# Splitting the first weight load of a decode-attention kernel into one third and the rest

## The chip, the cores and the metric

The kernel runs on one core of a Trainium2 chip. The metric is the device time of one execution in microseconds. A profiled execution also has a span (243.8 us for the kernel before), from its first to its last instruction; it is some 1.5 us shorter than the time. The profile's names: PE is the matmul engine and PEld its weight load, DVE, ACT and POOL are the other compute engines, SP issues the large loads. A load *lands* when its last byte is there. A ratio is the mean time of one kernel's fast runs over that of the other's in the same rounds on the same chip, so it is not quite the ratio of the medians that are quoted.

## The reference, cut to what matters

Two independent attention layers, A and B, decode one token each. A attends to the last 2048 positions of its cache, B to all 8192.

```python
Hq, Hkv, Sk, Dh = 32, 16, 8192, 128          # x has 576 elements
q = (x @ wq)                                  # wq: 576 x 4096
k, v = caches, each of 16 heads repeated for 2 query heads   # A: last 2048 rows only
p = softmax(q @ k.T * Dh ** -0.5)
out = (p @ v) @ wo                            # wo: 4096 x 576
# result: concatenate([A, B])
```

There is one query row per head, so there is little to compute for each byte: the inputs that must be read are 102.8 MB.

## The kernel before

All large inputs are loaded by one queue (SP), in a fixed order: wq of A, wq of B, keys and values of A, then keys and values of B in four groups, then wo of A and of B. The buffers are reused, so later loads wait until PE has read what stood there. wq of A is one load: 128 partitions, and in each one run of 18,432 elements (36,864 bytes).

```python
    def load(dst, src, writes, dma):
        add("sp", lambda sp: sp.dma_start(dst, src()), writes=writes, dma=dma)
    ...
    def q_part(P, off, res):                  # the projection x @ wq: 36 matmuls
        def mm(pe):
            for u in range(9):
                for j in range(4):
                    o = off + u * 2048 + j * 512
                    ins = pe.matmul(...rhs=slots[:, o:o + 512], start=(u == 0), stop=(u == 8))
            return ins
        add("pe", mm, reads=[("xpad", P)] + res, ...)     # waits for all of res first
    ...
    for P in range(2):                        # 0 is A, 1 is B
        off, res = WQ[P]
        x_columns(P)
        load(slots[:, off:off + WQ_W], lambda P=P: wqs[P]..., res, "wq%d" % P)
        q_part(P, off, res)
        q_finish(P)
```

The very first load of the program is moved ahead of the barrier with which the engines start together; all other loads are issued behind it:

```python
        first = per["sp"].pop(0)
        ...
        lead.insert(at, ins)                  # before the barrier
```

Of the kernel before, what the change touches and what calls it, by code (L numbers as in the profile page):

```python
# [20 lines left out]
WQ_W = 18432  # L21
# [15 lines left out]
class Program:  # L37
# [15 lines left out]
    def add(self, eng, fn, reads=(), writes=(), dma=None, after=(), tag=None, inc=1, loop=None):  # L53
        op = Op(eng, fn, tuple(reads), tuple(writes), dma, tag, inc if dma is None or inc > 1 else 16, loop)
        deps = []
        for r in op.reads:
            w = self.writer.get(r)
            if w is not None:
                deps.append((w, True))
            if r[0] == "bank":  # L60
                deps += [(o, False) for o in self.readers.get(r, ())]
        for r in after:
            deps += [(o, False) for o in self.readers.get(r, ())]
        for r in op.writes:
            w = self.writer.get(r)
            if w is not None:
                deps.append((w, False))
            deps += [(o, False) for o in self.readers.get(r, ())]
        for r in op.reads:
            self.readers.setdefault(r, []).append(op)  # L70
        for r in op.writes:
            self.writer[r] = op
            self.readers[r] = []
        for o, raw in deps:
            if o is op:
                continue
            if o.dma is None and o.eng == eng and (not raw or eng in ("pe", "sp")):
                continue
            op.deps.append(o)
            o.needed = True  # L80
        op.order = len(self.ops)
        self.ops.append(op)
        return op
# [192 lines left out]
def bass_concat_heads__sliding_block_cached__gqa_block_cached__decode_kernel(  # L276
# [16 lines left out]
    wqs = [A_wq, B_wq]  # L293
# [16 lines left out]
    slots = nc.alloc_sbuf_tensor("slots", [128, 4 * SLOT], BF16)  # L310
# [86 lines left out]
    def load(dst, src, writes, dma):  # L397
        add("sp", lambda sp: sp.dma_start(dst, src()), writes=writes, dma=dma)  # L398
# [49 lines left out]
    def x_columns(P):  # L448
        for u, n, col, i, e in ((0, 5, 0, 0, 0), (0, 5, 1, 4, 1), (1, 4, 0, 5, 1), (1, 4, 1, 0, 0)):
            dst = bass.AP(tensor=xpad, offset=(P * 9 + u) * 32 + col, ap=[[576, 128], [64, n]])  # L450
            add("dve", lambda dve, dst=dst, o=320 + 9 * P + i, n=n, e=e: dve.tensor_scalar(
                dst, misc[:, o:o + n], par2[:, e:e + 1], None, ALU.mult),
                reads=[B_M, "par2"], writes=[("xpad", P)])

    def q_part(P, off, res):
# [4 lines that stand above are left out]
                    ins = pe.matmul((turned if P else opsum)[32 * j:32 * j + 32, :], lhsT=xpad[:, P, u, :],  # L460
                                    rhs=slots[:, o:o + 512], start=(u == 0), stop=(u == 8))
            return ins
        add("pe", mm, reads=[("xpad", P)] + res, writes=[B_T if P else B_O])

    def q_finish(P):
        add("act", lambda act: act.activation(qrow[:, :], (turned if P else opsum)[:, :], ACT.Copy),  # L466
            reads=[B_T if P else B_O], writes=["qrow"])

        def tr(pe):
            for i in range(4):  # L470
                ins = pe.matmul(misc[:, i * 8:(i + 1) * 8], lhsT=qrow[:, i * 128:(i + 1) * 128],  # L471
                                rhs=selq[:, :, :].rearrange("p j h -> p (j h)"), start=True, stop=True)
            return ins
        add("pe", tr, reads=["qrow", "selq"], writes=[B_M])
        add("dve", lambda dve: dve.tensor_copy(qcol[:, P, :].rearrange("p (h j i) -> p i j h", h=2, j=4),  # L475
                                               misc[:, 0:32].rearrange("p (i j h) -> p i j h", i=4, j=4)),
            reads=[B_M], writes=[("qcol", P)])
# [236 lines left out]
    for P in range(2):  # L714
        off, res = WQ[P]
        x_columns(P)
        load(slots[:, off:off + WQ_W], lambda P=P: wqs[P].rearrange("(m r) n -> m (r n)", m=64)
             .rearrange("m (e y) -> (m e) y", e=2), res, "wq%d" % P)
        q_part(P, off, res)
        q_finish(P)  # L720

    sums(kindA[:, :].rearrange("p (b y) -> p b y", b=4), identf[:, :].rearrange("p (a b c y) -> p b y a c", a=2, b=4, c=2),
# [96 lines left out]
```

## Time and profile before

| what | value |
|---|---|
| time, median of 3 runs | 245.35 us (245.17 to 245.45) |
| span of the profiled run | 243.8 us |
| bytes moved | 102.88 MB, 422 GB/s over the span |
| share of the span in which the load queue's packets run | 98.3% |
| busiest compute engine | PE, 67% |

Compare the share of the load queue with that of the busiest engine: 98 against 67.

### The profile page before, as it was taken

The page shows a single profiled execution, that of the slowest core. Times are in us where ns is not written, and L with a number is a line of the kernel's source. Part 1 is how long each engine was busy: PE and PEld are TensorE (multiplying, and loading weights), DVE is VectorE, ACT ScalarE, POOL GpSimd, SP SyncE. Part 2 cuts the span into 40 slices and gives each one's busy share as a digit, 9 for nine tenths or more (in the row PEclk, how much of TensorE's full clock was granted, in tenths as well). Part 3 has the DMA queues.
Part 4 walks back from the last instruction along what each step waited for, and adds up shares of the span by engine and source line. Part 5 has one row for each costly group of instructions (what it writes and reads, how often), then busy time and mean ns, then how long its engine had stood idle before and what let it go on. Part 6 is the DMA issues. An engine that isn't in the chain of part 4 may idle for free. (4 is left out here: it accounts for less than half of the span.)

```text
span 243.8 us, 5219 instructions
## 1 busy us (share of the span) xinstructions
PE 164.0 (67%) x2328; PEld 119.3 (49%) x2328; DVE 88.2 (36%) x152; ACT 93.2 (38%) x96; POOL 6.8 (3%) x34
## 2 busy tenths in 40 slices
PE   0060739957249997393999452999457699944966
PEld 0020239744217784233887220987233688634854
DVE  0101127866205655203556312456322255534031
ACT  2000017855304776202778300678600368730000
POOL 6001000000000000000000000000000000000000
PEclk9999967999759999569899859799957589985599
DMA  9999999999999999899999999999989999989994
GB/s 351 424 442 403 430 433 422 430 425 427 449 427 433 485 398 462 371 435 430 485 409 452 419 403 435 435 489 398 473 366 430 435 489 419 462 374 423 422 406 175
DMA packets 3968, 102.88 MB, mean 422 GB/s; under 512 B 500, under 2 KB 632, under 8 KB 888
## 3 DMA queue, kind: packets, MB, share of 16 engines
q1 hardware_dynamic: 3896, 102.76, 98.3%
q8 instruction: 6, 0.10, 0.2%
q10 hardware_dynamic: 64, 0.00, 0.0%
q14 instruction: 2, 0.02, 0.0%
HBM read 102.76 MB, written 0.00 MB: 422 GB/s over the span
## 5 line engine op out<-in xcount | busy, mean ns | idle before, releaser
L510 ACT ACTIVATE kt<-ktps 128x1024 bf16<-128x1024 bf16 x80 | 79.8, 1042 | 87.5 <-PE ktps L500 87.3
L500 PE MATMUL ktps<-ident,slots 128*128 128x128 bf16 x1280 | 86.0, 231 | 19.9 <-PEq L214 17.4
L500 PEld LDWEIGHTS ktps<-ident,slots 128*128 128x128 bf16 x1280 | 79.8, 104 | 35.5 <-issue 35.4
L513 DVE COPY kt<-ktps 128x1024 bf16<-128x1024 bf16 x80 | 60.8, 774 | 54.5 <-PE ktps L500 54.5
L592 PE MATMUL opsum<-slots,ptm 128*32 128x512 bf16 x320 | 27.0, 510 | 13.4 <-PEq L214 13.4
L525 PE MATMUL sacc<-kt,qst 128*32 128x512 bf16 x320 | 25.4, 392 | 2.3 <-PEq L214 2.3
L592 PEld LDWEIGHTS opsum<-slots,ptm 128*32 128x32 bf16 x320 | 13.5, 124 | 25.5 <-issue 22.6
L563 PE MATMUL misc<-ident,psb 128*128 128x128 bf16 x40 | 4.7, 290 | 15.8 <-PEq L214 15.8
L610 DVE TENSOR_TENSOR vtmp<-opsum,maskV 128x512 f32<-128x512 f32 x4 | 2.8, 692 | 32.4 <-PE opsum L592 32.4
L551 ACT ACTIVATE psb<-sacc,stat 128x2048 bf16<-128x2048 f32 x5 | 9.8, 1967 | 9.7 <-DVE stat L540 9.7
L563 PEld LDWEIGHTS misc<-ident,psb 128*128 128x128 bf16 x40 | 3.5, 128 | 18.2 <-issue 18.2
L570 DVE TENSOR_TENSOR ptm<-misc,maskP 128x1024 bf16<-128x1024 bf16 x5 | 3.5, 691 | 16.1 <-PE misc L563 16.1
L525 PEld LDWEIGHTS sacc<-kt,qst 128*32 128x32 bf16 x320 | 5.0, 94 | 8.4 <-issue 4.7
L707 ACT ACTIVATE outsb<-ktps 64x144 bf16<-64x144 f32 x1 | 0.3, 287 | 20.2 <-PE ktps L695 20.2
L460 PE MATMUL turned<-slots,xpad 128*32 128x512 bf16 x36 | 4.0, 630 | 5.9 <-DMA slots<-in_B_wq_dram 5.9
L441 PE MATMUL misc<-xnine,twice 16*128 16x18 bf16 x4 | 0.3, 171 | 11.0 <-DMA xnine<-in_B_x_dram 11.0
L695 PE MATMUL ktps<-slots,opj 128*32 128x144 bf16 (+1 forms) x192 | 6.7, 247 | 0.8 <-issue 0.7
L475 DVE CAST qcol<-misc 128x32 bf16<-128x32 f32 x2 | 0.6, 300 | 17.2 <-PE misc L471 17.2
L695 PEld LDWEIGHTS ktps<-slots,opj 128*32 128x32 bf16 x192 | 5.4, 96 | 2.0 <-issue 0.9
L485 POOL COPY qst<-qcol 128x32 bf16<-128x32 bf16 x8 | 1.7, 211 | 152.2 <-PE sacc L525 152.2
L466 ACT ACTIVATE qrow<-opsum 128x512 bf16<-128x512 f32 x1 | 0.6, 597 | 13.8 <-PE opsum L460 13.8
L460 PE MATMUL opsum<-slots,xpad 128*32 128x512 bf16 x36 | 4.0, 630 | 2.6 <-DMA slots<-in_A_wq_dram 2.6
(77 smaller groups left out, 56.9 us busy)
## 6 DMA issues: line engine op xcount, KB each, us to landing
slots<-in_B_k_cache_dram SPq DMA_DIRECT2D x8, 4096.0 KB
slots<-in_A_k_cache_dram SPq DMA_DIRECT2D x4, 2048.0 KB
slots<-in_A_v_cache_dram SPq DMA_DIRECT2D x4, 2048.0 KB
slots<-in_A_wq_dram SPq DMA_DIRECT2D x1, 4608.0 KB, 13.9
slots<-in_B_wq_dram SPq DMA_DIRECT2D x1, 4608.0 KB, 23.9
slots<-in_A_wo_dram SPq DMA_DIRECT2D x1, 4608.0 KB, 18.7
slots<-in_B_wo_dram SPq DMA_DIRECT2D x1, 3024.0 KB, 25.5
slots<-in_B_wo_dram SPq DMA_DIRECT2D x1, 1008.0 KB, 7.7
```

Of the source, the lines that this page charges most:

```text
L460: ins = pe.matmul((turned if P else opsum)[32 * j:32 * j + 32, :], lhsT=xpad[:, P, u, :], rhs=slots[:, o:o + 512], start=(u == 0), stop=(u ...
L485: return pool.tensor_copy(dst, src)
L500: ins = pe.matmul(ktps_bf[q][:, t * 128:(t + 1) * 128], lhsT=slots[:, o:o + 128], rhs=ident[:, :], start=True, stop=True, is_transpose=True)
L510: add("act", lambda act, src=src, dst=dst: act.activation(dst, src, ACT.Copy), reads=[("bank", q)], writes=[("kt", u % NKT, q)], tag="e%d% ...
L513: add("dve", lambda dve, src=src, dst=dst: dve.tensor_copy(dst, src), reads=[("bank", q)], writes=[("kt", u % NKT, q)], tag="e%d%d" % (u, q))
L525: ins = pe.matmul(sacc[32 * j:32 * j + 32, :], lhsT=qst[:, o:o + 32], rhs=rhs, start=(u == 0 and e == 0), stop=True, skip_group_check=True)
L551: return act.activation(dst, src, ACT.Exp, bias=st(C_NB + g), scale=SCALE, accum_out=st(C_L + g))
L563: ins = pe.matmul(dst[:, t * 128:(t + 1) * 128], lhsT=psb[:, o:o + 128], rhs=ident[:, :], start=True, stop=True, is_transpose=True)
L570: return dve.tensor_tensor(ptm[:, c * 1024:(c + 1) * 1024].rearrange("p (t y) -> p t y", t=8), dst.rearrange("p (t y) -> p t y", t=8), mas ...
L592: ins = pe.matmul(opsum[64 * j + 32 * x:64 * j + 32 * x + 32, :], lhsT=ptm[:, o:o + 32], rhs=v[:, at[0], at[1], :, :, b:b + 128], start=(n ...
L610: add("dve", lambda dve: dve.tensor_tensor(vtmp[:, :, :], src, by, ALU.mult), reads=[B_O, w], writes=["vtmp"], tag="keep")
L695: ins = pe.matmul(ktps[P + j // 2][32 * j:32 * j + 32, 0:w], lhsT=opj[:, P, at:at + 32], rhs=slots[:, o:o + w], start=(jj == 0), stop=(jj ...
```

## The change

wq of A comes in two transfers, still over all partitions: the first third of each run (12,288 bytes) and then the other two thirds (24,576 bytes). The apparent intent is a quicker start: the load ahead of the barrier is short. The projection still waits for both.

```diff
-        load(slots[:, off:off + WQ_W], lambda P=P: wqs[P]..., res, "wq%d" % P)
-        q_part(P, off, res)
+        parts = [(0, WQ_W // 3, ["third"]), (WQ_W // 3, WQ_W, res)] if P == 0 else [(0, WQ_W, res)]
+        for lo, hi, what in parts:
+            load(slots[:, off + lo:off + hi], lambda P=P, lo=lo, hi=hi: wqs[P]...[:, lo:hi], what, "wq%d%d" % (P, lo))
+        q_part(P, off, [r for _, _, what in parts for r in what])
```

More of the change, by code (lines that the diff above doesn't have):

```diff
@@ L716, in bass_concat_heads__sliding_block_cached__gqa_block_cached__decode_kernel @@
         x_columns(P)
-        load(slots[:, off:off + WQ_W], lambda P=P: wqs[P].rearrange("(m r) n -> m (r n)", m=64)
-             .rearrange("m (e y) -> (m e) y", e=2), res, "wq%d" % P)
-        q_part(P, off, res)
+        parts = [(0, WQ_W // 3, ["third"]), (WQ_W // 3, WQ_W, res)] if P == 0 else [(0, WQ_W, res)]
+        for lo, hi, what in parts:
+            load(slots[:, off + lo:off + hi], lambda P=P, lo=lo, hi=hi: wqs[P].rearrange("(m r) n -> m (r n)", m=64)
+                 .rearrange("m (e y) -> (m e) y", e=2)[:, lo:hi], what, "wq%d%d" % (P, lo))
+        q_part(P, off, [r for _, _, what in parts for r in what])
         q_finish(P)
```

## The prediction

> **What bounds the kernel now.** I read the page of the profile first, and in it the slices of the span, because they show which resource has no free tenth.
>
> ```profile
> span 243.8 us, 5219 instructions
> ...
> PE 164.0 (67%) x2328; PEld 119.3 (49%) x2328; DVE 88.2 (36%) x152; ACT 93.2 (38%) x96; POOL 6.8 (3%) x34
> ...
> DMA  9999999999999999899999999999989999989994
> GB/s 351 424 442 403 430 433 422 430 425 427 449 427 433 485 398 462 371 435 430 485 409 452 419 403 435 435 489 398 473 366 430 435 489 419 462 374 423 422 406 175
> ...
> q1 hardware_dynamic: 3896, 102.76, 98.3%
> ```
>
> No compute engine is over 67% busy. The 16 transfer engines are at 90% or more in all but three slices, and the packets of the queue that all large loads use take 98.3% of the span of 16 engines, 239.7 of 243.8 us. The four microseconds that remain must be the start and the end, and the second view, stretches of my choice, shows that they are (columns: stretch, its length, busy time of PE, PEld, DVE, ACT and POOL, clock, DMA share, GB/s; a packet's bytes are counted where it starts).
>
> ```profile
> 0.00:1.00 1.00, 0.00 (x0) 0.00 (x0) 0.00 (x0) 0.00 (x0) 0.40 (x6) 1.00 0.00 0
> 1.00:2.00 1.00, 0.00 (x0) 0.00 (x0) 0.00 (x0) 0.02 (x1) 1.00 (x6) 1.00 1.88 553
> 2.00:3.00 1.00, 0.00 (x0) 0.00 (x0) 0.00 (x0) 1.00 (x1) 1.00 (x6) 1.00 0.30 111
> 3.00:14.00 11.00, 0.36 (x8) 0.29 (x12) 1.08 (x6) 0.47 (x2) 1.64 (x6) 1.00 1.00 429
> 14.00:34.00 20.00, 8.48 (x80) 2.72 (x78) 3.02 (x18) 1.19 (x2) 1.06 (x8) 0.97 1.00 432
> ...
> 238.00:241.00 3.00, 2.30 (x107) 1.99 (x105) 0.45 (x1) 0.00 (x0) 0.00 (x0) 1.00 0.75 291
> 241.00:243.80 2.80, 1.18 (x49) 0.67 (x41) 0.30 (x1) 0.29 (x1) 0.00 (x0) 1.00 0.07 21
> ```
>
> Nothing moves for one microsecond; from 3 us the rate is 429 to 437 GB/s in every long stretch, so no later part of the kernel starves the queue, whatever PE waits for there. The kernel is one unbroken stream of 102.9 MB with a start of some 2 us and an end of some 3 us. Third, the chain that ended last: its final links are a wait for a transfer and what follows from it.
>
> ```profile
> 233.15 0.04 issue
> 233.19 8.42 DMA slots<-in_B_wo_dram
> 241.61 0.04 issue
> 241.65 0.64 PE ktps L695 x16
> ```
>
> The last output weights are issued at 232.8 us and land at 241.6, 8.4 us later, because megabytes stand before them in the queue. Last, the instructions in order of time and the issues by transfer, for the part that the change touches:
>
> ```profile
> 0.00 0.41 SPq L398 DMA_DIRECT2D slots<-in_A_wq_dram  x1
> 0.80 0.35 SPq L398 DMA_DIRECT2D slots<-in_B_wq_dram  x1
> ...
> 11.01 0.25 PE L441 MATMUL misc<-xnine,twice 16*128 16x18 bf16 x4 [11.01 <-DMA xnine<-in_B_x_dram]
> ...
> 13.89 4.03 PE L460 MATMUL opsum<-slots,xpad 128*32 128x512 bf16 x36 [2.64 <-DMA slots<-in_A_wq_dram]
> ```
>
> The query projection of A starts at 13.89 us, when wq of A has landed, and needs 4.03 us; that of B starts at 24.78 us, when wq of B has landed. Neither is the bound: PE next works on keys at 34.6 us, when those have landed.
>
> **What the Trainium skill says.** "DMA: Bandwidth & Descriptors", section "Where 436 GB/s comes from", gives a ceiling of 435.2 GB/s for the 16 ports of a core. The trace agrees: the long stretches run at 427 to 437, so the middle of the kernel can't get faster without fewer bytes, and the change keeps every byte. The same page, "Queues, rings and completion order", says that an engine goes round its queues a whole packet at a time. The trace agrees: x is 1.1 KB, issued at 0.8 and 1.2 us on another queue, and takes 7.4 and 9.7 us to land, since each of its small packets stands behind a packet of wq of 36,864 bytes (1.364 us in the packet records). The section "Rules for kernel authors" asks for 128 partitions and at least 1 MiB for a transfer; the first third has 1.57 MB over 128 partitions, so neither part falls under it. No page says whether a short first transfer starts the engines sooner.
>
> **The change part by part.** *Order.* By the order of instructions, nothing moves on PE, DVE, ACT or POOL. SP issues one more transfer: the third goes out first, before the barrier; the other two thirds follow after it, at about 0.8 us, and all later issues come some 0.4 us later. Those for wq of B and the first keys have over 10 us of queued data before them, so their delay is hidden. The third itself, 1.57 MB at 432 GB/s, holds the engines for 3.6 us from about 1.3 us; what is issued at 0.8 us is there by about 2 (the first took 1.0 to 2.0), so no hole arises.
>
> *PE's wait.* The projection waits for both transfers before its first matmul. It isn't split, so it can't begin on the first third: it still starts when the last byte of wq of A is there, near 13.9 us. Even 4 us gained there would gain nothing, as PE then waits for wq of B and for keys.
>
> *Added cost.* Each engine carries 8 of the 128 rows. A row was one packet of 36,864 bytes and becomes one of 12,288 and one of 24,576: 8 more data packets and one more semaphore write for each engine. From the packet records, 65,536 bytes take 2418 ns and 16,384 take 611, so 36.8 ns for each 1000 bytes and 8.7 ns fixed; some 5 ns lie between packets. 9 packets by 14 ns is 0.13 us on each engine, and as the stream is unbroken, all of it reaches the end: +0.13 us.
>
> *Possible gain.* Only the start can change. The records show the first packets of the 16 engines beginning between 1.03 and 2.01 us, and taking 1.40 to 2.44 us instead of 1.364: 0.63 us too much in the mean. No later packet of wq is slow. If that excess goes with the size of the packet, two thirds vanish, -0.42 us; if it is a fixed latency of the first access, nothing does. For the first: the instruction fetches of 8 KB before the start took 0.34 to 0.53 us where the fit gives 0.31, an excess of 0.03 to 0.22 us only. Against it: some engines have nearly none (40 ns) with the same size, so size alone doesn't make it. I take half: -0.2 us. The sum is -0.07 us, under the spread of the three runs (0.28 us).
>
> **The rivals.**
> 1. *The early start is a real gain.* Small first packets bring all engines into step sooner. The finish times of the engines differ by 0.98 us at the end of wq of A, and the difference is kept through the stream, so the latest engine sets the end. If the first packets cost neither their excess nor their spread, the end comes up to 0.63 + 0.4 us earlier: 244.3 us. That is the best I can make of it, 0.4%.
> 2. *x comes sooner, and with it the start of compute.* x does come sooner: its rounds stand behind packets of about 0.46 us instead of 1.36, so I expect L441 between 5.5 and 8 us instead of at 11.0. But its product, xpad, is ready at 11.9 us now and isn't wanted before 13.9. Worth 0: 245.4 us without any other gain, 0.13 us of packets included.
> 3. *The split costs more than its packets.* If the engines ran dry between the third and the rest, for instance because the second issue waits for the barrier, a hole of up to 1 us would be pushed to the end: 246.4 us. The 3.6 us of work in the third speak against it, and the 0.80 us at which the second issue now goes.
> 4. *A stray shift of instruction fetches.* A fetch of 16 KB occupies one transfer engine about 1 us (six in the page's queue lines), and the engine that is hit becomes the latest. One more instruction on SP and one more wait on PE could move a fetch to another engine: plus or minus 0.5 us.
>
> **Range and chances.** From 245.35 us the sum gives 245.3, and I lean a little to rival 1, which has a signed hint in the records: 245.2 us. Rival 1 in full reaches 244.3 and rival 3 in full 246.4; half of either, with the spread of the runs, makes 244.5 to 245.9. Two per cent is 4.9 us, more than the whole start of 2 us that the change can touch and five times the hole of rival 3. Faster by 2% has one chance in a hundred, slower one, within 98.
>
> **What would show it.** Right: the span within 0.7 us of 243.8; the same 427 to 437 GB/s in the long stretches; the projection of A at 13.5 to 14.3 us with two transfers to wait for; L441 well before 11 us; 136 to 150 more packets in the queue line (128 rows and 16 semaphore writes are 144); the same final chain. It would be wrong if the second slice showed a hole in the stream, if the keys' first use came over half a microsecond away from 34.6 us, or if the stretches after 34 us ran at another rate: then the change reaches something that I hold to be out of its reach.

## The result, and the profile after

| kernel | median of 6 runs | range |
|---|---|---|
| before | 245.37 us | 245.17 to 245.45 |
| changed | 245.28 us | 245.16 to 245.34 |

The ratio is 0.9998, with a 95% interval of 0.9985 to 1.001: the same. Later runs sharpen this a little. There are 11 runs of the changed kernel and 20 of the kernel before from the same two jobs. Compared within each job, the changed kernel's mean is 0.06 us lower in the first and 0.09 us in the second; weighted together that is 0.08 us with a standard error of 0.04 us. If this is a gain, it is 0.03%. It isn't clear of the noise: within the second job, two sets of runs of the unchanged kernel differ by 0.09 us.

These are the slices of the changed kernel's page, as shown for the kernel before.

```profile
span 243.8 us, 5220 instructions
...
PE 164.1 (67%) x2328; PEld 119.3 (49%) x2328; DVE 88.3 (36%) x152; ACT 92.9 (38%) x96; POOL 6.8 (3%) x34
...
DMA  8999999999999999899999999999989999989994
...
q1 hardware_dynamic: 4040, 102.76, 98.3%
```

There is one instruction more, and there are 4040 - 3896 = 144 packets more, as many as 128 rows and 16 semaphore writes make. The share of the queue is unchanged. The same stretches as before (columns as in the prediction):

```profile
1.00:2.00 1.00, 0.00 (x0) 0.00 (x0) 0.00 (x0) 0.11 (x1) 1.00 (x6) 1.00 0.98 246
2.00:3.00 1.00, 0.00 (x0) 0.00 (x0) 0.00 (x0) 1.00 (x1) 1.00 (x6) 1.00 0.97 406
3.00:14.00 11.00, 0.78 (x12) 0.50 (x16) 1.08 (x6) 0.38 (x2) 1.64 (x6) 1.00 1.02 437
14.00:34.00 20.00, 7.51 (x80) 2.64 (x71) 3.02 (x18) 1.20 (x2) 1.07 (x8) 0.64 1.00 430
...
90.00:150.00 60.00, 41.90 (x558) 28.91 (x555) 21.71 (x32) 23.64 (x24) 0.64 (x3) 0.80 0.99 426
...
212.00:238.00 26.00, 16.57 (x204) 13.37 (x196) 7.36 (x23) 2.27 (x3) 0.00 (x0) 0.74 0.97 416
238.00:241.00 3.00, 1.91 (x112) 1.72 (x112) 0.00 (x0) 0.00 (x0) 0.00 (x0) 1.00 0.77 304
```

The first stretches look different, 246 and 406 GB/s for 553 and 111, but that is mostly bookkeeping: a packet's bytes are counted where it starts, and the packets are now smaller. From 14 us on the rates are the same within 3 GB/s up to 238 us. These are two of the later stretches in the kernel before, which the prediction leaves out:

```profile
90.00:150.00 60.00, 41.10 (x572) 28.50 (x568) 22.10 (x33) 24.01 (x25) 0.63 (x3) 0.83 0.99 427
...
212.00:238.00 26.00, 17.39 (x206) 13.60 (x205) 7.63 (x24) 3.09 (x4) 0.00 (x0) 0.74 0.97 419
```

The instructions in order of time show what came earlier in the changed kernel:

```profile
0.00 1.16 SPq L398 DMA_DIRECT2D slots<-in_A_wq_dram  x2
...
1.21 0.54 SPq L398 DMA_DIRECT2D slots<-in_B_wq_dram  x1
...
7.99 0.25 PE L441 MATMUL misc<-xnine,twice 16*128 16x18 bf16 x4 [7.99 <-DMA xnine<-in_B_x_dram]
...
13.47 3.48 PE L460 MATMUL opsum<-slots,xpad 128*32 128x512 bf16 x36 [5.24 <-DMA slots<-in_A_wq_dram]
```

x arrives 3.0 us sooner (L441 at 7.99 instead of 11.01) and only lengthens the wait that follows: PE now sits idle for 5.24 us ahead of the projection instead of 2.64. The projection starts 0.42 us sooner; that of B starts at 24.34 instead of 24.78, and the first work on keys at 34.23 instead of 34.67. (That this projection took 3.48 us instead of 4.03 is not the change's doing: a second profile of the same kernel has 4.03.) So at 34 us the changed kernel is 0.4 us ahead. The end of the chain that ended last tells what became of this lead:

```profile
231.12 10.45 DMA slots<-in_B_wo_dram
241.57 0.04 issue
241.62 0.64 PE ktps L695 x16
```

The last weights land at 241.57 us instead of 241.61. Nearly the whole lead of 0.4 us is gone. The link is a wait of 10.45 instead of 8.42 us because the load was issued two microseconds sooner into a queue that was as full as before; it landed no sooner for that. Where the lead went is the question for the experiments.

**A second reading: the 16 transfer engines one by one.** A transfer over 128 partitions is shared by 16 engines, 8 rows each, and each engine writes to the semaphore when it is done. The packet records of the trace hold these 16 writes, so one can list when each engine finished a given load. The mean of the 16 times is called the *mean landing* below. For the two profiles, in microseconds:

| load | first engine | mean | last engine | last minus first |
|---|---|---|---|---|
| wq of A, before | 12.51 | 12.85 | 13.48 | 0.98 |
| wq of A, changed | 12.49 | 12.75 | 13.03 | 0.54 |
| 3.0 MB of wo of B, near the end, before | 235.60 | 236.46 | 237.61 | 2.02 |
| the same, changed | 235.65 | 236.47 | 237.50 | 1.85 |

A load is complete when its last engine is done, and that came 0.45 us sooner for wq of A but only 0.11 us sooner near the end. In the kernel before the distance from the first to the last engine stays at 0.98 us for every load up to 34 us, but in both kernels it grows to about 2 us between 38 and 80 us.

### The profile page after: what moved, and what is told of

It reads as the page before. It is cut to its first block, busy times and chain, and to the rows that moved or that the text cites. A ratio compares the mean times of both kernels' runs of the same rounds, so it can differ in the third digit from the quotient of the medians.

```text
span 243.8 us, 5220 instructions
## 1 busy us (share of the span) xinstructions
PE 164.1 (67%) x2328; PEld 119.3 (49%) x2328; DVE 88.3 (36%) x152; ACT 92.9 (38%) x96; POOL 6.8 (3%) x34
## 3 DMA queue, kind: packets, MB, share of 16 engines
q1 hardware_dynamic: 4040, 102.76, 98.3%
## 5 line engine op out<-in xcount | busy, mean ns | idle before, releaser
L460 PE MATMUL opsum<-slots,xpad 128*32 128x512 bf16 x36 | 3.5, 559 | 5.2 <-DMA slots<-in_A_wq_dram 5.2
L441 PE MATMUL misc<-xnine,twice 16*128 16x18 bf16 x4 | 0.3, 171 | 8.0 <-DMA xnine<-in_B_x_dram 8.0
```

The costliest lines, as they stand in the source:

```text
L460: ins = pe.matmul((turned if P else opsum)[32 * j:32 * j + 32, :], lhsT=xpad[:, P, u, :], rhs=slots[:, o:o + 512], start=(u == 0), stop=(u ...
```

## The experiments

Three groups: what the start and the split are worth (first four), what a packet costs and what sets the end (next four), and controls with one more size (last three). My theory was the prediction's: an unbroken stream, of which the change touches only the start. All eleven runs gave correct results.

### tiny_first: a first part that is too short

```diff
-        parts = [(0, WQ_W // 3, ["third"]), (WQ_W // 3, WQ_W, res)] if P == 0 else ...
+        parts = [(0, WQ_W // 36, ["third"]), (WQ_W // 36, WQ_W, res)] if P == 0 else ...
```

> The changed kernel with a first part of one thirty-sixth (131 KB, rows of 1 KB) in place of a third. It holds an engine for 8 packets of some 51 ns, 0.4 us, less than the time from one issue to the next (0.8 us). If the transfer behind the barrier can leave a hole (my rival 3), wq of A lands 0.3 to 0.8 us later than with the third (13.5 us) and the time is 245.5 to 246.0 us. If the first packet's excess only shrinks with its size and no hole arises, wq of A lands at 13.2 to 13.5 us and the time is 245.0 to 245.3 us.

Measured: 245.97 us against 245.34 for before, ratio 1.0025 (1.0012 to 1.0039). The records show the hole. The engines finished the tiny part between 1.43 and 1.77 us, and the packets of the second transfer, issued behind the barrier, began between 1.79 and 2.77 us. Instructions in order of time:

```profile
0.00 1.16 SPq L398 DMA_DIRECT2D slots<-in_A_wq_dram  x2
...
14.47 4.03 PE L460 MATMUL opsum<-slots,xpad 128*32 128x512 bf16 x36 [5.03 <-DMA slots<-in_A_wq_dram]
```

The issues stand as in the changed kernel, and yet the projection starts one microsecond later (14.47 for 13.47). The mean landing of wq of A is 13.58 us. Against the mean of 12.94 us over all seven profiles that have wq of A whole, this is +0.64 us, and the time rose by 0.60 us in the mean. So a delay of the whole stream at its start reaches the end in full, and rival 3 exists: it takes a first part that is shorter than the wait for the second.

### two_thirds: the other way round

```diff
+        parts = [(0, 2 * WQ_W // 3, ["third"]), (2 * WQ_W // 3, WQ_W, res)] if P == 0 else ...
```

> The changed kernel with a first part of two thirds and then one third. The added packets are the same (0.13 us). If the excess of the first packets goes with their size, about two thirds of the 0.64 us stay and the mean landing of wq of A on the 16 engines comes within 0.1 us of the 12.85 us of before; if it is a fixed latency of each engine's first access, it comes 0.13 us later. The time is 245.2 to 245.5 us in both.

Measured: 245.32 us, ratio 0.9999 (0.9985 to 1.0012). The mean landing was 12.95 us, at the edge of the first expectation and just short of the second, and equal within 0.01 us to the 12.94 us of the whole load (mean of seven profiles). This run doesn't decide what the slow first packets depend on; it shows only that rows of 24 KB gain nothing.

### split_B: the added packets without the start

```diff
-        ... if P == 0 else [(0, WQ_W, res)]
+        ... if P == 1 else [(0, WQ_W, res)]
```

> wq of A whole as before; wq of B in a third and the rest. This has the added packets of the change without its effect at the start. By my sum the mean landing of wq of B is 0.13 us later than before (23.73 us) and the time is 245.4 to 245.5 us. If added packets cost nothing, the landing and the time are those of before (245.37 us).

Measured: 245.51 us, ratio 1.0004 (0.999 to 1.0018). The time can't tell this from nothing. The records can, if the start is taken out by the difference of the two landings: from the mean landing of wq of A to that of wq of B are 10.886 us in the kernel before and 10.929 us here. The nine added packets cost 0.043 us on an engine, 4.8 ns each, a third of what I had put.

### pe_split: let PE use the third

```diff
-        q_part(P, off, [r for _, _, what in parts for r in what])
+        for lo, hi, what in parts:
+            q_part(P, off, what, lo // 2048, hi // 2048)
```

> The change, with the projection of A split too: its first 12 matmuls wait for the first third alone, the other 24 for the rest. The projection should end near 16 us instead of 17.0 us. As PE then waits for wq of B (24.3 us) and for keys (34.2 us) all the same, I expect 245.2 to 245.4 us, as for the change. If the start of compute were on the path (rival 2), the time would fall by up to 1 us.

Measured: 245.28 us, ratio 0.9998 (0.9985 to 1.0012), as for the change. Instructions in order of time:

```profile
9.01 1.47 PE L460 MATMUL opsum<-slots,xpad 128*32 128x512 bf16 x12 [0.81 <-DVE xpad L451]
13.48 2.75 PE L460 MATMUL opsum<-slots,xpad 128*32 128x512 bf16 x24 [2.99 <-DMA slots<-in_A_wq_dram]
...
24.39 4.03 PE L460 MATMUL turned<-slots,xpad 128*32 128x512 bf16 x36 [7.20 <-DMA slots<-in_B_wq_dram]
```

PE does a third of the projection at 9 us and ends it near 16.2 us, and then waits for wq of B 7.20 us, until 24.39 us as before. The start of compute isn't on the path; rival 2 is worth nothing even when PE is let loose.

### B_18: the cost of a packet, multiplied

```diff
+        parts = [(k * 1024, k * 1024 + 1024, res if k == 17 else ["part%d" % k])
+                 for k in range(18)] if P == 1 else [(0, WQ_W, res)]
```

> The kernel before, with wq of B in 18 transfers of rows of 2 KB: the suspected cost of packets, multiplied. 17 times 9 more packets for each engine at 14 ns (8.7 fixed, some 5 between packets) are 2.1 us. If the stream is the bound and packets cost this, the time is 247.2 to 247.7 us; if the fixed cost hides behind the data, it stays at 245.4 us.

Measured: 246.95 us against 245.46, ratio 1.006 (1.0045 to 1.0076), so +1.5 us instead of 2.1. From the landing of wq of A to that of wq of B are 12.035 us, 1.149 more than before, over 153 added packets: 7.5 ns each. Packets do cost time in the stream, but half of what I had put. Of the +1.5 us, some 0.3 are not in this stretch; the runs spread over 0.5 us and I leave that open.

### one_engine_5us and one_engine_1us: load on one engine alone

```diff
+    load(kt[0:17, 0, 0:4096], lambda: vs[0][0, 0, 0:17 * 32, :].rearrange("(p t) d -> p (t d)", p=17), ..., "more")
```

The second kernel has rows of 1024 elements in place of 4096. The load goes to a buffer that isn't in use yet.

> The kernel before and, behind wq of B, one useless load of 139 KB in 17 rows of 8 KB, which should run on one transfer engine alone (17 rows can't be shared out). That engine gets 17 packets of some 315 ns, 5.35 us more. If the engine that is last sets the end, and the last is now some 2.0 us behind the first, the time rises by 3.3 to 4.4 us (by 5.35 if the engine is already one of the last). If the mean over the 16 engines counts, it rises by 5.35/16, 0.33 us.

> The same with rows of 2 KB: 17 packets of some 89 ns, 1.5 us more on one engine. If the last engine sets the end, an engine that was 0 to 0.5 us behind the first stays within the present 2.0 us and the time doesn't change (245.4 us); it rises by up to 0.5 us if the engine was up to 1 us behind, and by 1.5 us if it is one of the last. By the mean it rises by 0.09 us.

Measured: 252.4 us against 245.46 (ratio 1.0278, 1.0262 to 1.0294), and 245.67 us (ratio 1.0011, 0.9997 to 1.0025: the same). In the first, the time rose by 6.9 us in the mean, more than I had expected, because the load took longer: its 17 packets took 0.31 us each while they ran beside wq of B and up to 0.70 us beside the keys, and held their engine from 23.71 to 32.17 us, 8.46 us. Why they slowed isn't tested. The second load held its engine for 1.64 us (23.53 to 25.17); the mean time is 0.26 us higher, but the interval of the ratio includes 1.

By the mean over 16 engines the two would have cost 0.5 and 0.1 us. In the first run 6.9 us were paid, so all but 1.5 us of the 8.46 reached the end. In the second, the semaphore writes show that the loaded engine wasn't the last. When the second load of A's keys ended it was 1.87 us behind the first engine, and no other was more than 1.03 us behind. When wo of A ended, near 230 us, it was 1.90 us behind, but five others were 1.96 to 2.27 us behind (the controls below tell why). So if the 0.26 us are real, this engine's lateness isn't their cause. **A single engine was 1.64 us late without being the last at the end; of 8.46 us of lateness all but about 1.5 were paid.** That each microsecond beyond the slack costs a whole one is an estimate from the first run, as the slack depends on where the engine stands among the 16.

The page of the first shows the other engines run out of work while one is still busy:

```profile
DMA  9999999999999989899998999989999999999970
GB/s 358 394 464 401 387 419 428 423 430 428 438 433 442 381 365 501 360 444 428 433 497 386 428 423 438 496 365 480 391 423 433 417 506 438 397 385 424 418 274 29
```

Its last stretches (columns as before) are nearly empty for four microseconds:

```profile
245.00:249.00 4.00, 2.12 (x112) 1.75 (x112) 0.00 (x0) 0.00 (x0) 0.00 (x0) 1.00 0.12 43
249.00:251.20 2.20, 0.61 (x16) 0.29 (x16) 0.30 (x1) 0.29 (x1) 0.00 (x0) 1.00 0.01 1
```

### even_same_bytes: the same bytes on all engines

```diff
+    load(kt[:, 0, 0:544], lambda: vs[0][0, 0, 0:544, :]...(128 rows of 544 elements), ..., "more")
```

> The same 139 KB in 128 rows of 1 KB, which all 16 engines share: 8 packets of some 54 ns and a semaphore write for each engine, 0.44 us. The time rises by 0.3 to 0.5 us by either theory; beside the load on one engine it tells that these bytes alone do not cost microseconds.

Measured: 245.80 us, ratio 1.0012 (0.9999 to 1.0026), 0.33 us more in the mean. 139 KB cost some 0.3 us when shared (not clear of the noise) and 6.9 us on one engine: it is the latest engine that sets the end, not the bytes.

### before_again and after_again: controls

No edit; each kernel once more, with a profile and five rounds.

> The kernel before, unchanged, as a control for the small differences: 245.2 to 245.5 us. Its latest engine should finish wq of A at 13.2 to 13.5 us and the mean of the 16 at 12.85 to 13.0 us, as in the six profiles so far with wq of A whole; after the instruction fetches between 38 and 80 us the latest engine should be some 2.0 us behind the first, and an engine that a fetch has delayed, not the one that was last at the start.

> The changed kernel again, on the same chip as the control. If the start gain (0.17 us in the mean landing of wq of A, 0.3 us in the last) reached the end, the time would be 0.17 to 0.3 us under the control. If a part of it is lost because fetches make other engines the last, 0.0 to 0.15 us. The mean landing should again be near 12.77 us and the last near 13.05 us.

Measured: 245.47 us for before (ratio 1.0003 to its own other runs) and 245.33 us for the changed kernel (0.9998). In the seven profiles with wq of A whole its mean landing is 12.85 to 13.00 us (mean 12.94) and its last engine 13.23 to 13.48 (mean 13.35); in the three with the third first, 12.75 to 12.78 (mean 12.76) and 13.02 to 13.08 (mean 13.04). So the third does bring the start forward: 0.17 us in the mean, 0.31 us in the last engine, and the groups don't overlap. Of the 0.31 us, some 0.08 reach the time, which fits the second expectation of after_again. Near the end the same can be asked of the 3.0 MB of wo of B: its last engine finishes at 237.61 and 237.90 us in the two profiles of before, and at 237.50, 237.54 and 237.66 in the three with the third first. That is some 0.2 us, but these groups overlap, so the 0.11 us of the first pair isn't a firm number. At the end of wo of A the last engine is 2.35 us behind the first in before_again (2.0 was expected) and 1.99 in after_again.

These are the finish times of the 16 engines in the first profile of before, sorted, as distances in microseconds from the first. The load is the second one of A's keys (ends at 34 us), and wo of A (ends at 230 us):

```
34 us   0.00 0.08 0.14 0.15 0.17 0.18 0.24 0.24 0.27 0.37 0.40 0.42 0.51 0.58 0.72 0.98
230 us  0.00 0.14 0.16 0.17 0.24 0.27 0.36 0.60 0.60 0.96 1.01 1.72 1.75 1.78 2.00 2.02
```

Between them the records have four instruction fetches of 16 KB (at 38.1, 52.5, 67.7 and 73.5 us) and two of 8 KB (at 80.2 and 120.9). After the first, the next data packet of the engine is 0.54 us slow; with the fetch's own 1.02 us the engine loses 1.56 us. Five engines end up at 1.7 to 2.0 us, which fits four such losses on top of distances of 0.15 to 0.45 us, and about 1.0 us for one of the 8 KB fetches on top of 0.7. The engine that was last at the start, at 0.98, ends at 1.01: it is now a microsecond away from being last. To bring it forward is worth nothing. What counts, on this reading, is the start of the engines that fetches will hit; they were in the midst of the field and gained less. In the changed kernel's first profile the last at 230 us is 1.85 us behind, 1.57 more than an engine that was 0.28 behind at 34 us. In that profile each engine can be followed from packet to packet: the four that carried a 16 KB fetch between 38 and 72 us fell back by 1.53 to 1.57 us, the two with an 8 KB fetch (at 77.3 and 123.1 us) by 1.0 and 0.7, and the other ten kept their distances within 0.1 us. The four are the last four at 230 us. The five late engines of one_engine_1us fit too: distances of 0.40 to 0.72 us at 34 us and a 16 KB fetch, or 1.03 and an 8 KB fetch.

### sixth_first: a still smaller first part

```diff
+        parts = [(0, WQ_W // 6, ["third"]), (WQ_W // 6, WQ_W, res)] if P == 0 else ...
```

> The changed kernel with a first part of one sixth (786 KB, rows of 6 KB): 8 packets of some 231 ns, 1.85 us for an engine, still as long as the time until the packets of the second transfer come (1.8 to 2.8 us, seen with the tiny part), so no hole or hardly one. If smaller first packets help further, the mean landing of wq of A is 12.6 to 12.75 us and the time up to 0.1 us under the third's; if the large packets behind are as slow to begin as with the tiny part, or a hole begins, the landing is 12.8 to 13.0 us and the time 245.3 to 245.5 us.

Measured: 245.37 us, ratio 0.9999 (0.9985 to 1.0013); mean landing 12.88 us, last engine 13.31. It is hardly better than the whole load (12.94 and 13.35), as the second of its expectations had it, so the third is not improved on by going smaller. No run beat the changed kernel by more than the noise.

## Why the prediction was right, and where it wasn't

**The bound.** Right. The long stretches kept their rates, an added delay of 0.64 us came out as 0.60 us (tiny_first), and an earlier start of compute came out as nothing (pe_split). Two readings slipped on the way: four slices are under 90%, not three, and the stretches from 90 and from 212 us ran at 427 and 419 GB/s in the kernel before, so "429 to 437 in every long stretch", and later 427 to 437, leave them or one of them out. What bears the argument is that each stretch keeps its rate (426 and 416 after the change).

**PE's wait.** Right. The projection starts at 13.47 us, a hair before the range I gave (13.5 to 14.3). x came at 7.99 us, at the very edge of 5.5 to 8, and was worth nothing.

**The added cost.** Mis-sized. I put 14 ns for a packet, 8.7 from the fit and 5 between packets. The runs have 4.8 ns (split_B) and 7.5 ns (B_18). The 5 ns must not be added: in the records of rows of 2 KB (B_18) a packet most often lasts 84 ns but the next one starts 80 ns after it, so packets overlap rather than leave gaps. The term is 0.04 us instead of 0.13.

**The gain at the start.** The size was right: 0.17 us net in the mean landing, and with 0.04 us of packets 0.21 us, where I took 0.2. The reason stays open. I halved between an excess that goes with the size of the packet and a fixed latency; neither fits all runs. Rows of 24 KB (two_thirds) gained nothing, rows of 6 KB (sixth_first) less than 12 KB, and behind the tiny part the large packets were slow again (1.85 to 2.42 us for all but one of the first sixteen, where later ones have 1.33), although every engine had moved data already. That speaks against a latency of the first access alone.

**Rival 1's step "the difference is kept through the stream, so the latest engine sets the end".** Half of it failed. The latest engine does set the end: the loads on one engine show it. But the latest at the end isn't the latest at the start. Fetches between 38 and 80 us push other engines past it, and the gain of 0.31 us in the last engine of wq of A became some 0.08 us in the time. That the fetches set engines back is read off the records, engine by engine; that this is where the gain went is argued from them, not shown by a run that removed the fetches. That was not tried.

**The sum.** -0.07 us was predicted, -0.08 with a standard error of 0.04 was measured. This is closer than the terms deserve, and partly luck: a cost that was too high and a gain that was only partly paid out nearly cancelled. The lean to rival 1, 245.2 us, went a little too far: 245.28 was measured. Three small slips don't bear on it: rival 2's 245.4 us is 245.5 by its own terms (245.35 + 0.13), the upper end of 245.9 us leaves out the spread that the lower end has in it, and the 8.4 us of the last weights count from the end of their issue (8.8 from its start at 232.8).

**Rival 4** in its own form made nothing visible: both kernels have the same number of fetches, at times that differ by up to 3 us (38.1 and 38.0, 67.7 and 65.1 us), and the last engine is some 2 us behind in both.

## What to carry to other kernels

When one queue is busy for 98% of the span, a change to the start can be worth at most what the start costs, here 2 us of 245; look that up before asking anything else. A transfer over all partitions is done when its slowest engine is done, so list the 16 engines' finish times: lateness of one engine is free up to its distance to the last at the end (1.64 us were free here), and most of what lies beyond is paid (6.9 of 8.46 us). A split of the first load needs a first part that lasts until the second one arrives: here a part with rows of 1 KB left a hole and cost 0.6 us, parts with rows of 6 and 12 KB cost nothing visible.

## What the Trainium skill lacked or had wrong

- "DMA: Bandwidth & Descriptors": no section says when the engines of one core begin relative to each other. Here the first packets began between 1.03 and 2.01 us in the kernel before, the first and the last finish of wq of A lay 0.5 to 1.0 us apart in all thirteen profiles, and in the kernel before the distance stayed at 0.98 us for every load up to 34 us.
- The same page, "Measured (HBM→SBUF, 128 partitions, SWDGE, issued from GpSimd)", gives about 10.5 ns for a packet, for loads issued from GpSimd. Packets added to a running stream from SP cost 4.8 to 7.5 ns here.
- "Runtime: NRT & Kernel Launch", "Instruction fetch mechanics", calls the cost of crossing a block of 16 KB mostly hidden. It speaks of the instruction stream; for the loads it isn't hidden here: such a fetch set one transfer engine back by 1.53 to 1.57 us, and engines set back so were the last to finish.
- No page says that rows of a load that one engine alone carries may slow down beside other traffic: packets of 8 KB took 0.31 us and, from 25 us on, up to 0.70 us.
